# A build-time planner that tries eight orders of each step, and counts less time between engines

## The chip, the cores and the metric

The kernel runs on one core of a Trainium2 chip. The metric is the device time of one execution in microseconds: the median of several runs, 1663.62 us for the kernel before (four runs, 1661.84 to 1665.83 us). A core has a matrix engine (PE, TensorE), a vector engine (DVE, VectorE), an activation engine (ACT, ScalarE), a general engine (POOL, GpSimd) and a queue engine that starts DMAs (SP, SyncE). Each runs its own list of instructions strictly in order and waits on semaphores where it needs another's result. So the order in which the program puts the instructions on each engine decides who waits for whom.

## The reference

Linear attention without softmax, a norm of every row of 64, and then a mixture of four experts whose weights are given per row. All is in float32.

```python
kv = np.einsum('bhsd,bhse->bhde', k, v)        # B, H, S, D = 8, 8, 576, 64
out = np.einsum('bhsd,bhde->bhse', q, kv)
rms = np.sqrt(np.mean(out * out, axis=-1, keepdims=True) + 1e-06)
x = out / rms * g_norm                          # then (B,H,S,D) -> (B*S, H*D) = (4608, 512)
p = domain_probs / (domain_probs.sum(-1, keepdims=True) + 1e-09)
for e in range(4):                              # w1: (4, 512, 1024), w2: (4, 1024, 512)
    h = np.maximum(x @ w1[e], 0.0)
    out += p[:, e:e + 1] * (h @ w2[e])
```

## The kernel before

**The work.** The 4608 rows are cut into nine chunks of 512: the first 512 rows of each of the eight batches, and a ninth that gathers the last 64 rows of all of them. An expert times a chunk is a step, `s = e * 9 + c`, so there are 36 steps. A step multiplies up (rows by `w1[e]`, then a ReLU) and down (by `w2[e]`, then times the row's probability and added to the output). Both products are done in a Strassen-like scheme of seven products of halves instead of eight, applied once or twice, so DVE, POOL and ACT have to form sums and differences of blocks before and after. In expert 0 the attention of the next batch is worked in between: `key_values` (L999) forms kv, `attend` (L1024) multiplies by q, `turn_x` (L1069) transposes the normed rows with the help of an identity matrix. Step 0 is plain: `up_plain` (L1331) multiplies up without the scheme.

**The PSUM banks** matter here. PE writes only to PSUM, which is cut into eight banks: two each of the kinds `u1`, `u2`, `db` and `ab`. PE can't write a bank again before ACT or DVE have taken the previous result out of it. An up product of the scheme (L1244) writes `u1` or `u2` and is copied out by ACT (L1265) or added up by DVE (L1273). A down product writes `db` or `ab`, and ACT (L1409, L1579) or DVE (L1416, L1587) take it. `attend` needs two `ab` banks and two `db` banks at once; they are emptied by `evacuate` (L920 on DVE, L921 on ACT). `turn_x` needs both `ab` banks, emptied by ACT at L1081.

**The order.** None of this is written out in its final order. The kernel adds some 8,500 operations to a `Plan`, each with a key (its step and its place in the step), a cost for each engine that could do it, and the buffers that it reads and writes. `layout` then plays the program through at build time. At each moment it asks every engine that is free for an operation. On PE and SP the first ready one in order of the key is taken; on DVE, ACT and POOL the ready one with the earliest due time is taken. Due times run backwards from PE's order: what PE needs earlier is due earlier. An operation counts as ready only when every input has been finished for `CROSS` (0.3 us) if another engine made it, or for `SAME` (0.06 us) if the same one did; a bank or buffer is free again `CROSS` after its last use. The chip does not use these numbers: it waits on semaphores. They only shape the order. `layout` runs once.

**Fillers.** While the opening (batch 0's attention and the first loads) leaves PE without work, `layout` puts in idle pairs of transposes of the identity (L1715), two matmul instructions of 128 columns each. They compute nothing that is used. They are put only where the next real PE operation has a key below zero, which holds for the opening alone.

**The helper lines.** L410 is every half-array matmul of the scheme, L433 every sum or difference of blocks in SBUF, L439 every load.

Of the kernel before, what the change touches and what calls it, by code (L numbers as in the profile page):

```python
# [39 lines left out]
class Plan:  # L40
# [11 lines left out]
    CROSS, SAME, LANES = 0.3, 0.06, 8  # L52
# [5 lines left out]
    SLOW = 6.8  # L58
    SHARED, AHEAD, INORDER = ("big",), 0.3, ("xf",)
# [31 lines left out]
    def layout(self, slots, later, idle, idle_banks, idle_until):  # L91


        free = {k: [(0.0, i) for i in range(len(v))] for k, v in slots.items()}
        slots = {k: list(v) for k, v in slots.items()}
        later = list(later)
        live = {}
        for b in {b for op in self.ops for b in op.bufs}:
            live[b.kind] = live.get(b.kind, 0) + 1
        ended = {}  # L100
        todo = {e: [] for e in self.REACH}
        for n, op in enumerate(self.ops):
            op.n = n
            for e in op.cost:
                todo[e].append(op)
        for e in todo:
            todo[e].sort(key=lambda o: (o.key, o.n))
        keys, begun, spent = [], [], 0.0
        for op in todo["PE"]:
            keys.append(op.key)  # L110
            begun.append(spent)
            spent += op.cost["PE"]
# [8 lines left out]
        missing, after = {}, {op: [] for op in self.ops}  # L121
        for op in self.ops:
            missing[op] = len(op.deps)
            for d in op.deps:
                after[d].append(op)
        waiting = {k: {} for k in self.SHARED}

        def arm(op):
            for b in op.outs:
                if b.kind in waiting and b.slot is None and "SP" not in op.cost:  # L130
                    waiting[b.kind][op] = max([d.end for d in op.deps] or [0.0])

        for op in self.ops:
            if not missing[op]:
                arm(op)
        first, known = {k: {} for k in self.INORDER}, set()
        for op in self.ops:
            for b in op.outs:
                if b.kind in first and b not in known:
                    known.add(b)  # L140
                    first[b.kind][op] = True

        def claimed(kind, op):
            return sum(
                1 for o, since in waiting[kind].items()
                if o.due < op.due and since <= t + self.AHEAD and o is not op
            )

        busy = {e: 0.0 for e in todo}
        bus, port = 3.8, 0.0  # L150
        lanes = [0.0] * self.LANES
        t = 0.0
        wake = [0.0, 1.6]
        left = len(self.ops)
        order = []

        def ready(op, eng):
            when = 0.0
            for d in op.deps:
                if d.start is None:  # L160
                    return None
            for d in op.deps:
                when = max(when, d.end + (self.SAME if d.eng == eng else self.CROSS))
            need = {}
            for b in op.outs:
                if b.kind is not None and b.slot is None:
                    need[b.kind] = need.get(b.kind, 0) + 1
            for k, n in need.items():
                spare = self.SPARE.get(k, 0) if k != "xf" or op.key < self.FORMS else 0
                ahead = op.key > front + 0.1 and (eng == "SP" or op.early)  # L170
                if len(free[k]) < n + (spare if ahead else 0):
                    return None
                if k in waiting and len(free[k]) < n + claimed(k, op):
                    return None
                if k in first and any(o.due < op.due for o in first[k] if o is not op):
                    return None
                when = max(when, sorted(free[k])[n - 1][0])
            if eng == "SP":
                when = max(when, lanes[0])
            if op.port:  # L180
                when = max(when, port)
            return when

        while left:
            moved = False
            while todo["PE"] and todo["PE"][0].start is not None:
                todo["PE"].pop(0)
            front = todo["PE"][0].key if todo["PE"] else 1e9
            for eng in todo:
# [8 lines left out]
                best = None  # L198
                kept = {}
                for op in pending:  # L200
# [8 lines left out]
                    when = ready(op, eng)  # L209
# [9 lines left out]
                    best = op  # L219
                    if eng in ("PE", "SP"):  # L220
                        break
                if best is not None:
                    op = best
                    op.start, op.eng = t, eng
                    if eng == "SP":
                        busy[eng] = t + op.cost[eng]
                        bus = max(bus, t + 1.5) + op.kb / 215.0
                        op.end = bus + 0.5
                        lanes = lanes[1:] + [op.end]
                    else:  # L230
                        op.end = busy[eng] = t + op.cost[eng]
                        if op.kb:
                            op.end += 9.0 if op.kb == 512 else 8.0
                    if op.port:
                        port = op.end
                        heapq.heappush(wake, port)
                    for b in op.outs:
                        if b.kind is not None and b.slot is None:
                            free[b.kind].sort()
                            b.slot = free[b.kind].pop(0)[1]  # L240
                            b.ap = slots[b.kind][b.slot]
                    for held in list(waiting.values()) + list(first.values()):
                        held.pop(op, None)
                    for o in after[op]:
                        missing[o] -= 1
                        if not missing[o]:
                            arm(o)
                    for b in op.bufs:
                        b.left -= 1
                        if b.left == 0 and b.kind is not None:  # L250
                            end = max(o.end for o in [op] + b.readers + b.writers) + self.CROSS
                            free[b.kind].append((end, b.slot))
                            live[b.kind] -= 1
                            ended[b.kind] = max(end, ended.get(b.kind, 0.0))
                            for rule in [r for r in later if not any(live.get(k) for k in r[0])]:
                                later.remove(rule)
                                end = max(ended[k] for k in rule[0])
                                for ap in rule[2]:
                                    free.setdefault(rule[1], []).append((end, len(slots[rule[1]])))
                                    slots[rule[1]].append(ap)  # L260
                                heapq.heappush(wake, end)
                    heapq.heappush(wake, busy[eng])
                    heapq.heappush(wake, op.end + self.SAME)
                    heapq.heappush(wake, op.end + self.CROSS)
                    order.append(op)
                    left -= 1
                    moved = True
                if eng == "PE" and busy[eng] <= t and 1.6 <= t and front < idle_until:
                    kind, spare = next((
                        (k, f) for k in idle_banks for f in free[k] if f[0] <= t  # L270
                    ), (None, None))
                    if spare is not None:
                        took = 0.43 if t < self.SLOW else 0.23
                        op = Op(front, {"PE": took}, None, (), (), 0, False)
                        op.start, op.eng, op.end = t, eng, t + took
                        op.fn = lambda eng, bank=slots[kind][spare[1]]: idle(bank)
                        busy[eng] = op.end
                        free[kind].remove(spare)
                        free[kind].append((op.end, spare[1]))
                        heapq.heappush(wake, op.end)  # L280
                        order.append(op)
                        moved = True
            if moved:
                continue
            while wake and wake[0] <= t:
                heapq.heappop(wake)
            assert wake, ("no operation can start", t, left, {
                e: (todo[e][0].key, todo[e][0].fn) for e in todo if todo[e]
            }, {k: len(v) for k, v in free.items()})
            t = heapq.heappop(wake)  # L290
        self.length = max(o.end for o in order)
        return order
# [1473 lines left out]
```

## Time and profile before

| what | value |
|---|---|
| median of the runs | 1663.62 us |
| the profiled execution's own time | 1661.9 us |
| its span, first to last instruction | 1659.7 us |
| PE busy | 1650.9 us (99% of the span) |
| DVE busy | 1283.5 us (77%) |
| ACT busy | 976.3 us (59%) |
| POOL busy | 648.4 us (39%) |
| granted PE clock | 1.00 |

PE is busy nearly all the time, so the span is PE's work plus the time in which PE stands still. PE's work is the same set of products in any order; what an order can change is the fillers and the places where PE waits. "Start us, us" in a timeline are start and duration of a merged group of instructions of one line; a bracket tells how long the engine had been idle and what ended it. A matmul's duration reaches past the start of the next, since they overlap in the pipeline; so the time from one group's start to the next group's start is the better measure of what it costs.

### The profile page before, as it was taken

The page shows a single profiled execution, that of the slowest core. Times are in us where ns is not written, and L with a number is a line of the kernel's source. Part 1 is how long each engine was busy: PE and PEld are TensorE (multiplying, and loading weights), DVE is VectorE, ACT ScalarE, POOL GpSimd, SP SyncE. Part 2 cuts the span into 40 slices and gives each one's busy share as a digit, 9 for nine tenths or more (in the row PEclk, how much of TensorE's full clock was granted, in tenths as well). Part 3 has the DMA queues.
Part 4 walks back from the last instruction along what each step waited for, and adds up shares of the span by engine and source line. Part 5 has one row for each costly group of instructions (what it writes and reads, how often), then busy time and mean ns, then how long its engine had stood idle before and what let it go on. Part 6 is the DMA issues. An engine that isn't in the chain of part 4 may idle for free.

```text
span 1659.7 us, 66359 instructions
## 1 busy us (share of the span) xinstructions
PE 1650.9 (99%) x28884; PEld 1558.8 (94%) x28884; DVE 1283.5 (77%) x2153; ACT 976.3 (59%) x2420; POOL 648.4 (39%) x649
## 2 busy tenths in 40 slices
PE   9999999999999999999999999999999999999998
PEld 6688888888899999999999999999999999999996
DVE  4778777766888687888788887888888887788874
ACT  3455555554556665666666666666666666666662
POOL 3532323214344554333355445433355444433332
PEclk9999999999999999999999999999999999999999
DMA  9876865624466444444558444444577544444442
GB/s 215 192 227 183 228 181 145 167 101 181 160 175 149 112 117 119 115 114 113 141 161 194 115 117 118 103 116 117 137 185 179 129 116 117 106 114 116 117 104 52
DMA packets 208123, 234.27 MB, mean 141 GB/s; under 512 B 97368, under 2 KB 148440, under 8 KB 207832
## 3 DMA queue, kind: packets, MB, share of 16 engines
q1 hardware_dynamic: 184760, 193.32, 38.8%
q0 software_dynamic: 23072, 36.71, 14.6%
q8 instruction: 227, 3.72, 0.9%
q14 instruction: 64, 0.52, 0.1%
HBM read 155.79 MB, written 74.19 MB: 139 GB/s over the span
## 4 chain that ended last, share of the span: by engine, by line
PE 99%; DMA 0%; DVE 0%; ACT 0%; issue 0%; SPq 0%; ACTq 0%; DVEq 0%
PE u L410 48%; PE db L410 32%; PE ab L410 15%; PE ab L1004 1%; PE ab L1031 1%; PE ab L1072 1%; DMA big<-in_q_dram 0%; PE ab L1715 0%; PE db L1040 0%; PE ab L753 0%; PE ab L772 0%; PE ab L1093 0%; PE ab L817 0%; SPq L439 0%; DVE ss L944 0%
## 5 line engine op out<-in xcount | busy, mean ns | idle before, releaser
L433 DVE TENSOR_TENSOR big<-big,big 128x1024 f32<-128x1024 f32 (+1 forms) x518 | 503.1, 985 | 41.2 <-ACT big L1229 17.6
L410 PE MATMUL u<-xf,big 128*64 128x128 f32 x7072 | 507.9, 273 | 0.2
L410 PEld LDWEIGHTS u<-xf,big 128*64 128x64 f32 x7072 | 410.5, 137 | 5.7 <-issue 1.7
L410 PE MATMUL u<-xf,w1y 128*64 128x128 f32 x5304 | 384.1, 273 | 0.0
L410 PE MATMUL db<-big,big 128*64 128x128 f32 (+1 forms) x4320 | 361.1, 307 | 1.4 <-ACT snap L921 1.4
L1273 DVE TENSOR_TENSOR big<-u,snap 128x256 f32<-128x256 f32 x458 | 192.0, 421 | 174.3 <-PE u L410 137.5
L410 PEld LDWEIGHTS u<-xf,w1y 128*64 128x64 f32 x5304 | 308.9, 137 | 3.3 <-issue 0.3
L1265 ACT ACTIVATE snap<-u 128x256 f32<-128x256 f32 x490 | 188.0, 384 | 197.6 <-PE u L410 159.7
L410 PEld LDWEIGHTS db<-big,big 128*64 128x64 f32 x4320 | 265.0, 137 | 40.7 <-ACT snap L921 1.6
L433 POOL TENSOR_TENSOR big<-big,big 128x256 f32<-128x256 f32 (+1 forms) x166 | 196.9, 1190 | 156.4 <-DVE big L433 92.3
L1265 ACT ACTIVATE big<-u 128x256 f32<-128x256 f32 x458 | 175.0, 384 | 90.3 <-PE u L410 64.5
L433 POOL TENSOR_TENSOR big<-big 128x512 f32<-128x512 f32 (+1 forms) x79 | 94.8, 1201 | 148.7 <-DVE big L433 95.4
L1579 ACT ACTIVATE snap<-db 128x256 f32<-128x256 f32 (+1 forms) x230 | 82.4, 358 | 101.5 <-PE db L410 93.5
L1229 ACT ACTIVATE big<-big 128x1024 f32<-128x1024 f32 x131 | 137.7, 1051 | 5.5 <-DVE big L433 2.7
L433 DVE TENSOR_TENSOR big<-big 128x512 f32<-128x512 f32 (+1 forms) x128 | 111.3, 878 | 0.0
L1265 ACT ACTIVATE u<-u 128x256 f32<-128x256 f32 x245 | 91.0, 371 | 31.1 <-PE u L410 14.8
L1617 POOL TENSOR_TENSOR big<-big 128x512 f32<-128x512 f32 x28 | 35.7, 1276 | 184.3 <-DVE big L433 168.5
L1432 POOL DMA_DIRECT2D out_dram<-big x100 | 89.5, 1126 | 46.1 <-ACT big L1409 31.4
L410 PE MATMUL db<-small,big 128*64 128x128 f32 x1416 | 106.4, 273 | 0.4 <-ACT snap L1579 0.4
L1587 DVE TENSOR_TENSOR big<-ab,snap 128x256 f32<-128x256 f32 x160 | 67.2, 420 | 38.8 <-PE ab L410 25.6
L410 PE MATMUL ab<-big,big 128*64 128x128 f32 (+1 forms) x1344 | 93.6, 278 | 0.0
L410 PE MATMUL db<-kv,big 128*64 128x128 f32 x1264 | 87.4, 273 | 0.0
(193 smaller groups left out, 2343.3 us busy)
## 6 DMA issues: line engine op xcount, KB each, us to landing
xf<-x SPq DMA_DIRECT2D x108, 512.0 KB, 3.7
out_dram<-big POOLq DMA_DIRECT2D x84, 256.0 KB, 5.6
xf<-x_h SPq DMA_DIRECT2D x81, 256.0 KB, 3.3
xf<-x SPq DMA_DIRECT2D x81, 256.0 KB, 3.7
x<-xf SPq DMA_DIRECT2D x36, 512.0 KB, 4.7
big<-in_moe_w_dram SPq DMA_DIRECT2D x31, 512.0 KB, 5.3
x_h<-big SPq DMA_DIRECT2D x18, 512.0 KB, 4.1
big<-in_moe_w_dram POOLq DMA_DIRECT2D x17, 512.0 KB, 6.5
```

The costliest lines, as they stand in the source:

```text
L410: nc.tensor.matmul(out_[cols], lhsT=lhsT[:, cols], rhs=rhs, **kw)
L433: lambda eng: adder(eng).tensor_tensor(out=out_(), in0=a(), in1=b(), op=op),
L1004: nc.tensor.matmul(bank.ap[r * D:(r + 1) * D, o * D:(o + 1) * D], lhsT=ks[r], rhs=vs[r], start=(j == 0), stop=(j == len(sets) - 1), skip_g ...
L1031: nc.tensor.matmul(raw[r].ap[c * D:(c + 1) * D, (o * NR + t) * D:(o * NR + t + 1) * D], lhsT=qt.ap[half, col:col + D], rhs=kv.ap[half, o * ...
L1072: nc.tensor.transpose(turned[o].ap[:, r * P:(r + 1) * P], qt.ap[:, o * NT + r * P:o * NT + (r + 1) * P], ident[:])
L1229: lambda eng: nc.scalar.activation(out=b.ap[:], in_=b.ap[:], func=ACT.Relu),
L1265: lambda eng: nc.scalar.activation(out=where(), in_=ps.ap[:, 0:HN], func=ACT.Copy),
L1273: lambda eng: nc.vector.tensor_tensor(out=block(whole, a, t), in0=src.ap[:, 0:HN], in1=add_.ap[:], op=ALU.add),
L1432: nc.gpsimd.dma_start(out=dst, in_=cell(i)[parts, :], accum_op=ALU.add)
L1579: lambda eng: nc.scalar.activation(out=where(), in_=group_of(ps.ap), func=ACT.Copy),
L1587: lambda eng: nc.vector.tensor_tensor(out=cell(tq, dq), in0=group_of(src.ap), in1=group_of(add_.ap), op=ALU.add,),
L1617: lambda eng: adder(eng).tensor_tensor(out=whole(to), in0=whole(a), in1=whole(b), op=ALU.add),
```

## The change

Three things. `CROSS` goes from 0.3 to 0.2 us. `layout` no longer runs once: at each of the steps it saves its state, plays this step and the next eight times, and keeps the play in which PE stood still least (the planner's clock less the real PE work done, `self.t - self.worked`; fillers are not counted as work). Play 0 uses the due times as they are; plays 1 to 7 add to each due time of this step's and the next step's operations a random number of mean 0 and spread 1 us. Then the step is played once more with the chosen numbers, and the next step is searched. And for this the body of `layout` is moved into methods that can be stopped and restarted (`ready`, `claimed`, `run`, `begin`, `arm`). The rules of readiness, PE's "first ready in order of the key" and the costs are as before. No instruction of the chip is new, and nothing but the order, the buffers that operations get, the engine that an operation with a choice goes to, and the count of fillers can differ.

```diff
-    CROSS, SAME, LANES = 0.3, 0.06, 8
+    CROSS, SAME, LANES = 0.2, 0.06, 8
...
+    TRIES, LOOK, SPREAD = 8, 1, 1
...
+        for op in self.ops:
+            op.base = op.due
...
+        steps = {}
+        for op in self.ops:
+            steps.setdefault(math.floor(op.key), []).append(op)
+        for step in sorted(steps):
+            begin = self.save()
+            tried = []
+            for n in range(self.TRIES):
+                draw = random.Random(100 * n + step)
+                for op in steps[step] + steps.get(step + 1, []):
+                    op.due = op.base + (draw.gauss(0.0, self.SPREAD) if n else 0.0)
+                if self.run(step + 1 + self.LOOK):
+                    tried.append((self.t - self.worked, n))
+                self.restore(begin)
+            n = min(tried)[1]
+            draw = random.Random(100 * n + step)
+            for op in steps[step] + steps.get(step + 1, []):
+                op.due = op.base + (draw.gauss(0.0, self.SPREAD) if n else 0.0)
+            assert self.run(step + 1)
+        self.run(math.inf)
...
+    def run(self, until):
...
+            front = todo["PE"][0].key if todo["PE"] else 1e9
+            if front >= until:
+                return True
...
+    def begin(self, op, eng):
...
+        if eng == "PE":
+            self.worked += op.cost[eng]
```

## The prediction

> **What bounds the kernel now.** I read the page first: span, busy times, and the chain that ended last.
>
> ```profile
> span 1659.7 us, 66359 instructions
> PE 1650.9 (99%) x28884; PEld 1558.8 (94%) x28884; DVE 1283.5 (77%) x2153; ACT 976.3 (59%) x2420; POOL 648.4 (39%) x649
> PE 99%; DMA 0%; DVE 0%; ACT 0%; issue 0%; SPq 0%; ACTq 0%; DVEq 0%
> ```
>
> PE is the chain: 8.8 us of the span are not PE's. The busy times by stretch of time tell where these 8.8 us lie (second number of a row: PE).
>
> ```profile
> 0.00:16.00 16.00, 13.79 (x228) 12.05 (x230) 2.80 (x9) 6.26 (x13) 0.70 (x6) 1.00 0.93 221
> 16.00:32.00 16.00, 16.00 (x176) 9.20 (x170) 12.10 (x26) 5.55 (x14) 9.91 (x7) 1.00 0.89 222
> 32.00:66.00 34.00, 32.59 (x388) 15.76 (x388) 20.65 (x47) 13.77 (x39) 19.26 (x19) 1.00 0.99 206
> 66.00:120.00 54.00, 54.00 (x875) 44.65 (x876) 42.98 (x95) 28.37 (x71) 16.78 (x24) 1.00 0.80 219
> 120.00:1600.00 1480.00, 1479.65 (x26456) 1431.04 (x26454) 1173.59 (x1931) 901.26 (x2236) 587.42 (x581) 1.00 0.53 138
> 1600.00:1660.00 60.00, 54.88 (x780) 46.06 (x776) 31.42 (x48) 21.11 (x51) 14.29 (x12) 1.00 0.32 63
> ```
>
> 2.2 us are in the first 16 (the identity and the loads), 1.4 before 66, 0.35 in the 1480 us of the body, 5.1 at the end. Of the last, some 4.4 are the last sums and the output's DMA behind PE's last product. After the opening the waits of PE name two places:
>
> ```profile
> PE db L410 <- ACT snap L921: 1.4, 1, 1.4
> PE db L410 <- ACT snap L1579: 0.4, 1, 0.4
> ```
>
> Waits below 0.15 us beyond the pipeline's overlap are in no such list, so I also compared start to start. A scheme product takes 0.44 us from its start to the next one's. Where it is longer, PE waited:
>
> ```profile
> 179.78 0.66 PE L410 MATMUL u<-small,big 128*64 128x128 f32 x8
> 180.27 0.61 PE L410 MATMUL u<-xf,big 128*64 128x128 f32 x8
> 180.93 0.33 PE L410 MATMUL u<-small,big 128*64 128x128 f32 x2
> ```
>
> 180.27 to 180.93 is 0.66, so 0.22 of waiting. Four such places (147.1, 180.9, 251.3, 519.9 us) come to 0.22 + 0.22 + 0.30 + 0.21 = 0.95 us, and the place of 0.4 in the list is 0.54 by this measure (1628.85 to 1629.83 less 0.44). With the 1.42 at 61.3 us, **PE's waiting behind the opening is 2.9 us**. The last item that an order can change is filler work, which counts as busy:
>
> ```profile
> L1715 PE MATMUL ab<-ident 128*128 128x128 f32 x60 | 9.6, 316 | 1.4 <-POOL ident masks.py:199 1.4
> 30.87 1.31 PE ab L1715 x12
> ```
>
> Even a perfect order can't gain more than the 2.9 and the fillers behind the first real product. That bounds the gain at some 6 us, 0.36%. About 0.2% (3.3 us) is what a measurement of this kernel can tell from no change.
>
> **Part 1: fillers.** Both builds' orders are known before a run. The kernel before has 31 filler pairs (62 matmuls), the one after has 24 (48). The nine ahead of the first product are kept. The clearest loss is the block of twelve matmuls at 30.87 us, ahead of the second half of `up_plain`: PE waited there for ACT to take the last `turn_x` of batch 0 out, while one first-half product of `up_plain` (1.7 us) had already been spent. After, that product is placed behind the last `turn_x` and covers ACT's 0.69 us copy, so the block is gone. Fourteen matmuls at 1.31 / 12 = 0.109 us are **-1.53 us**. What covers this: the loads of `w1` must be there 1.5 us earlier. They land between 18.9 and 24.7 us; the first is needed at 21.5, the last not before 37, so the cover holds. If it did not, the fillers' time would turn into waiting, and the term would be 0.
>
> [...] I take -1.53.
>
> **Part 2: where PE will wait.** A product that reuses a bank has to wait for the round PE, ACT, PE. From the trace: a product placed at 144.35 is followed by the next at 144.78 and its ACT copy starts at 145.01, so 0.22 us from PE's slot to ACT; a copy ends at 145.69 + 0.37 and PE starts at 146.11, so 0.05 from ACT to PE. With a copy of 0.38 a bank is free 0.65 us after its product. In the order before, six PE operations stand less than 0.65 us of PE work behind the product whose bank or block they need, and five of the waits above are at these. In the order after there are seven, and most are others. Each, with durations from this trace:
>
> - `turn_x` of batch 1 is now directly followed by `attend` of its second half, which needs both `ab` banks. ACT first has two ReLU copies (0.22 + 0.66 from the start of `turn_x`), then two L1081 copies, 1.27 for both, and 0.05. That is 2.20, less 1.03 of `turn_x`: **1.17**.
> - That `attend`, then one product, then the first down product, which needs `db`. ACT starts 0.10 before `attend`'s end and does one copy (0.63 to the next), then two small ones (0.26, 0.27): 1.06, and 0.05, less 0.44: **0.67**. This takes the place of the 1.42.
> - A down product directly behind the user of its bank: 0.22 + 0.48 + 0.05: **0.75**.
> - `attend` of batch 2, one product, `turn_x`: DVE's copy of 0.69 starts 0.03 behind `attend`; 0.77 less 0.44: **0.33**.
> - `attend` of batch 4, directly followed by a down product on `db`: the 1.11 of the second item, uncovered: **1.11**.
> - The end of the last step but one, as before: **0.54** for two of the seven.
>
> The rows behind the `attend` items are these (L1031, L1040 are `attend`, 1.32 us from start to next start):
>
> ```profile
> 198.17 1.16 PE L1031 MATMUL ab<-kv,small 64*64 64x64 f32 x64
> 199.16 0.40 PE L1040 MATMUL db<-kv,small 64*64 64x64 f32 x8
> 199.39 0.60 ACT L921 ACTIVATE small<-ab 128x512 f32<-128x512 f32 x1 [0.68 <-PE ab L1031]
> 199.49 0.66 PE L410 MATMUL u<-xf,big 128*64 128x128 f32 x8
> 199.52 0.69 DVE L920 COPY small<-ab 128x512 f32<-128x512 f32 x1 [0.83 <-PE db L1040]
> 200.02 0.27 ACT L921 ACTIVATE snap<-db 64x128 f32<-64x128 f32 x1
> ```
>
> To these I add 0.5 us for waits through two engines (as at 147.1 before, where DVE's L944 was late), for which I see some five candidates and take 0.1 each, with 0 and 1.5 as ends. Sum 1.17 + 0.67 + 0.75 + 0.33 + 1.11 + 0.54 + 0.5 = 5.1, against 2.9 before: **+2.2 us**.
>
> **Part 3: the smaller count between engines.** 0.3 + 0.38 + 0.3 = 0.98 us kept a reuse of a bank three products away (1.31); 0.2 + 0.38 + 0.2 = 0.78 allows two (0.87). PE operations with less than 0.9 us of PE work behind their producer go from 80 to 343. The real round is 0.65, so each has 0.22 us to spare, and behind the waiting PE everything is queued. What eats the 0.22 is an ACT or DVE that is still at something else, such as a ReLU of 1.05 us (L1229). Before, none of the 74 such places that had these 0.22 us shows a wait. From none in 74 to 263 new ones: between 0 and some 11 waits of 0.2, so 0 to 2.2 us; I take **+0.3**, near the row that shows none. DVE, ACT and POOL have 376 us and more to spare in the span; that their work moves costs nothing beyond these waits. SP's loads are put by the same rules: before, no load made PE wait behind 16 us, and the closest ones after 60 us landed 0.2 us ahead of DVE. The order after keeps the same kinds of loads as the closest; 0, with -0 and +1 as ends.
>
> **The sum.** -1.53 + 2.2 + 0.3 = +1.0 us. The profiled execution's 1661.9 (span 1659.7 and 2.2 around it) becomes 1662.9. The median of the runs lies 1.7 above that execution, so the forecast is **1664.6 us**, no change that can be told.
>
> **The rivals.**
>
> *Faster (1659.8).* The planner's choice works: fillers -1.7, and the new waits shrink to some 0.8 since ACT takes the small `db` copies first. For it: the search counts just this idle time, and the real round is 0.13 below what even the new count supposes. Against: PE takes the first ready operation by key in all eight plays, so the search moves only the other engines, and the seven close places stand in the order as built. -1.7 - 2.1 = -3.8.
>
> *Slower (1669.5).* The two-product spacing fails in the repeating part. Steps 10 to 35 have much the same order, so a place where ACT is late is late in every step. Its place is the L1265 copy behind an L1229 ReLU, its price 0.2 us times 26 = 5.2 us; beside my +1.0 less 0.3 that is 1669.5. It decides from 2.4 us on, that is 0.09 us a step. For it: 263 places more with only 0.22 to spare. Against: no such wait before; ACT is busy 59%.
>
> *The change doesn't do what it says.* The planner's idle time is not the chip's: 0.98 of planned round against 0.65 real made it count waits that never were. Then it trades nothing for nothing, 1663.6; this falls into "no change".
>
> **How the numbers follow.** My forecast with the third rival: 0.67. Faster by over 0.2% (below 1660.3): 0.09. Slower by over 0.2% (above 1666.9): 0.24, the larger since one repeating wait is multiplied by 26. The range reaches from -3 (fillers -1.7, waits 2 shorter than summed, a median that falls 0.5 low) to +5.4 (the upper ends of parts 2 and 3, or the repeating wait): 1660.6 to 1669.0.
>
> **What would show it.** Right: 48 L1715 matmuls; the second half of `up_plain` starting near 30.5 instead of 32.1 us; PE waits named by L1081 and L921 or L920 between 55 and 65 us and near 200; body idle of 4 to 6 us start to start, none repeating by step. Wrong: PE waits on L1265 in step after step; a PE wait for a load; the granted clock below 1.00.

## The result and the profile after

The kernel after takes **1660.69 us** (median; 1659.57 to 1664.75), the kernel before, run beside it, 1662.79 (1660.89 to 1665.83). The ratio is 0.9988 with an interval of 0.9984 to 0.9992: **2.1 us less, between 1.3 and 2.7**. It is just inside the range (1660.6 to 1669.0) and still under the 0.2% that was named as the limit of what can be told, but its interval doesn't reach 1, and it points the other way than the forecast of +1.0. The time lies nearer to the rival "faster" (1659.8) than to the forecast (1664.6).

In the profile after, every line number of the kernel is 64 higher: L474 is the scheme's product (L410 before), L985 and L1145 are ACT's copies (L921, L1081), L1329 is ACT's copy of an up product (L1265), L1779 the fillers (L1715). First the page: span, busy times, and the chain that ended last.

```profile
span 1660.5 us, 66193 instructions
PE 1649.2 (99%) x28870; PEld 1557.1 (94%) x28870; DVE 1248.1 (75%) x2142; ACT 980.2 (59%) x2421; POOL 704.6 (42%) x659
PE 98%; DVE 1%; DMA 0%; ACT 0%; issue 0%; SPq 0%; POOL 0%; POOLq 0%; DVEq 0%; ACTq 0%
```

This execution (1662.37 us) is one of the longer ones of the kernel, and its span is longer than that of the one before (1659.7), while the medians say the opposite. One profile of each would have told the wrong sign. What can be read from it: PE's busy time is 1.7 us less, most of which is the fourteen fillers; DVE works 35 us less and POOL 56 us more, and neither has more than 1% of the chain. Busy times by stretch of time (the columns of the first such table; PE is the second number):

```profile
0.00:16.00 16.00, 14.15 (x220) 12.21 (x220) 2.10 (x8) 6.30 (x13) 0.70 (x6) 1.00 0.94 229
66.00:120.00 54.00, 52.84 (x870) 44.09 (x868) 42.87 (x91) 28.43 (x69) 24.39 (x28) 1.00 0.80 222
120.00:1600.00 1480.00, 1477.90 (x26426) 1428.57 (x26424) 1135.69 (x1923) 903.17 (x2235) 641.44 (x589) 1.00 0.53 138
```

PE stands still 1.2 us between 66 and 120 and 2.1 between 120 and 1600, where it had stood 0 and 0.35. The list of its waits, whole lines of that view, says for whom:

```profile
PE u L474 <- issue: 1.3, 1, 1.3
PE db L474 <- ACT snap L985: 1.1, 2, 0.8
PE db L474 <- ACT big L1473: 0.7, 1, 0.7
PE ab L1095 <- ACT big L1145: 0.7, 2, 0.4
PE ab L1136 <- DVE small L1017: 0.5, 1, 0.5
PE db L474 <- ACT snap L1643: 0.5, 1, 0.5
```

Most of the names are those that the prediction gave; L1017, on DVE, is not, and its 0.5 us are not in the list of `again`, the same order once more. The first line is a new kind, "issue": PE waited for nothing that the profile shows. A timeline of PE has its place:

```profile
145.46 0.27 PE L474 MATMUL u<-small,big 128*64 128x128 f32 x1
147.00 0.55 PE L474 MATMUL u<-small,big 128*64 128x128 f32 x6 [1.27 <-issue]
```

In the middle of a product, between two of its eight matmuls, 1.27 us are lost. Another execution of the same order (`again`, below) has no such wait in its list, so it belongs to the execution and not to the order. Without it, this profile's span would be 0.5 us under that of before.

### The profile page after: what moved, and what is told of

Same layout as the page of the kernel before. It is cut to its first block, busy times and chain, and to the rows that moved or that the text cites. A ratio compares the mean times of both kernels' runs of the same rounds, so it can differ in the third digit from the quotient of the medians.

```text
span 1660.5 us, 66193 instructions
## 1 busy us (share of the span) xinstructions
PE 1649.2 (99%) x28870; PEld 1557.1 (94%) x28870; DVE 1248.1 (75%) x2142; ACT 980.2 (59%) x2421; POOL 704.6 (42%) x659
## 4 chain that ended last, share of the span: by engine, by line
PE 98%; DVE 1%; DMA 0%; ACT 0%; issue 0%; SPq 0%; POOL 0%; POOLq 0%; DVEq 0%; ACTq 0%
PE u L474 47%; PE db L474 32%; PE ab L474 15%; PE ab L1068 1%; PE ab L1095 1%; PE ab L1136 1%; DMA big<-in_moe_w_dram 0%; PE ab L1779 0%; PE ab L817 0%; DVE big L497 0%; PE db L1104 0%; PE ab L1157 0%; DVE rt L700 0%; PE ab L836 0%; PE ab L881 0%
## 5 line engine op out<-in xcount | busy, mean ns | idle before, releaser
L497 DVE TENSOR_TENSOR big<-big,big 128x1024 f32<-128x1024 f32 (+1 forms) x544 | 515.4, 965 | 29.4 <-ACT big L1293 12.0
L474 PE MATMUL u<-xf,big 128*64 128x128 f32 x7072 | 513.0, 273 | 0.1
L474 PEld LDWEIGHTS u<-xf,big 128*64 128x64 f32 x7072 | 412.0, 137 | 5.4 <-issue 0.8
L474 PE MATMUL u<-xf,w1y 128*64 128x128 f32 x5304 | 393.3, 273 | 0.0
L474 PE MATMUL db<-big,big 128*64 128x128 f32 (+1 forms) x4280 | 359.2, 308 | 2.2 <-ACT snap L985 1.1
L1337 DVE TENSOR_TENSOR big<-u,snap 128x256 f32<-128x256 f32 x470 | 197.4, 421 | 204.1 <-PE u L474 153.8
L474 PEld LDWEIGHTS u<-xf,w1y 128*64 128x64 f32 x5304 | 310.9, 137 | 3.3 <-issue 0.8
L474 PEld LDWEIGHTS db<-big,big 128*64 128x64 f32 x4280 | 261.8, 137 | 43.2 <-issue 2.3
L1329 ACT ACTIVATE snap<-u 128x256 f32<-128x256 f32 x490 | 188.2, 384 | 189.1 <-PE u L474 165.3
L497 POOL TENSOR_TENSOR big<-big,big 128x256 f32<-128x256 f32 (+1 forms) x158 | 218.4, 1385 | 166.8 <-DVE big L497 72.8
L1329 ACT ACTIVATE big<-u 128x256 f32<-128x256 f32 x470 | 179.5, 384 | 64.3 <-PE u L474 38.4
L497 POOL TENSOR_TENSOR big<-big 128x512 f32<-128x512 f32 (+1 forms) x104 | 126.9, 1221 | 182.4 <-DVE big L497 110.1
L1293 ACT ACTIVATE big<-big 128x1024 f32<-128x1024 f32 x136 | 143.0, 1051 | 5.2 <-DVE big L497 4.4
L1329 ACT ACTIVATE u<-u 128x256 f32<-128x256 f32 x245 | 90.9, 371 | 38.4 <-PE u L474 26.2
L474 PE MATMUL db<-small,big 128*64 128x128 f32 x1312 | 98.7, 273 | 0.0
L474 PE MATMUL ab<-big,big 128*64 128x128 f32 (+1 forms) x1360 | 94.8, 278 | 0.0
L1473 ACT ACTIVATE big<-big,p_all 128x256 f32<-128x256 f32 x180 | 85.5, 501 | 0.4 <-POOL big L1681 0.2
L474 PE MATMUL ab<-kv,big 128*64 128x128 f32 x1232 | 85.1, 273 | 0.0
```

Source lines behind the costliest of these rows:

```text
L474: nc.tensor.matmul(out_[cols], lhsT=lhsT[:, cols], rhs=rhs, **kw)
L497: lambda eng: adder(eng).tensor_tensor(out=out_(), in0=a(), in1=b(), op=op),
L1293: lambda eng: nc.scalar.activation(out=b.ap[:], in_=b.ap[:], func=ACT.Relu),
L1329: lambda eng: nc.scalar.activation(out=where(), in_=ps.ap[:, 0:HN], func=ACT.Copy),
L1337: lambda eng: nc.vector.tensor_tensor(out=block(whole, a, t), in0=src.ap[:, 0:HN], in1=add_.ap[:], op=ALU.add),
L1473: lambda eng: nc.scalar.activation(out=cell(i, half), in_=ap(), func=ACT.Copy, scale=prob()),
```

## The experiments

Two profiles of one order differ by more than the effect (1662.37 us for `after`, 1659.88 for `again`), so two measures stand beside each other: medians of many runs, and a **ledger** from the traces. For the ledger each matmul's time to the next one's start is compared with the usual spacing of its form; what is beyond that, and every filler, is time lost to PE. Here "the opening" is the first 17 us of real work, and "the repeating part" is 300 to 1600. A loss is booked by how much real work PE had done by then, so that different orders are compared at the same stage. 17 us of real work are done near 29 us of the clock; the block of twelve fillers lies in "17-24". Neighbouring columns are exact to some 0.3 us only, since a change from one form of matmul to another can fall on either side of an edge; the sums don't depend on this. `body_only`, `refill` and `seed2` are left out, since their clock fell back for a while (last section); for `measured32` none was made.

```
real work done, us:   0-17  17-24  24-300  300-1600  1600-end   sum
before               12.24   1.58    6.13      1.01      0.76   21.7
neither              12.24   1.58    5.96      1.00      0.76   21.5
look_b               12.72   1.58    6.29      1.01      0.76   22.4
noblock              12.51   0.27    6.34      1.00      0.76   20.9
after (less 1.27)    11.91   0.00    7.98      0.53      0.84   21.3
again                11.04   0.00    7.64      0.53      0.84   20.1
look_a               11.55   0.00    7.33      0.53      0.84   20.3
look_a2              12.11   0.00    7.51      0.53      0.84   21.0
cross_only           13.20   0.00    7.51      3.42      0.84   25.0
search_only          13.10   1.58    6.36      0.67      0.76   22.5
open_only            11.62   0.00   11.17      0.83      0.76   24.4
c25                  10.83   0.00    7.36      2.80      0.84   21.8
nofill               12.30   0.00    9.44      0.53      0.84   23.1
tries32              11.68   0.00    8.13      0.55      0.84   21.2
```

Medians of the timed runs, with the ratio to the kernel before on the same chip (ratios are formed within rounds, so they needn't be the quotient of the medians):

```
              count  orders   median     before     ratio  [95%]
neither        0.3     1      1662.30    1662.42    0.9998 [0.9989, 1.0007]
cross_only     0.2     1      1664.08    1662.42    1.0008 [1.0000, 1.0017]
search_only    0.3     8      1662.19    1662.42    0.9992 [0.9984, 1.0001]
again          0.2     8      1660.33    1662.42    0.9986 [0.9978, 0.9995]
open_only      mixed   8      1663.03    1662.87    0.9997 [0.9988, 1.0006]
body_only      mixed   8      1663.33    1662.87    0.9999 [0.9990, 1.0008]
refill         0.2     8      1663.61    1662.87    1.0003 [0.9994, 1.0012]
c25            0.25    8      1663.64    1662.87    0.9998 [0.9990, 1.0007]
seed2          0.2     8      1661.56    1662.46    0.9997 [0.9989, 1.0006]
nofill         0.2     8      1660.45    1662.46    0.9988 [0.9980, 0.9997]
tries32        0.2     32     1662.26    1662.46    0.9997 [0.9989, 1.0006]
measured32     by pair 32     1661.41    1662.46    0.9992 [0.9983, 1.0000]
```

### The two halves of the change

All four corners of "smaller count" and "search". `neither` is the new code with both switched off; its order is that of the kernel before.

```diff
-    CROSS, SAME, LANES = 0.2, 0.06, 8
+    CROSS, SAME, LANES = 0.3, 0.06, 8
...
-    TRIES, LOOK, SPREAD = 8, 1, 1
+    TRIES, LOOK, SPREAD = 1, 1, 1
```

> The changed code with both numbers set back: 0.3 us between engines, one play per step. Its order is that of the kernel before, instruction by instruction. Both theories: 1662.8 us, within 0.5 of the kernel before. Its profile is a second look at that order: if the places where TensorE waits (61.3, 147, 181, 251, 520, 1630 us, 3.0 us in sum by start to start) are set by the order, they come back to within 0.3 us; what does not come back is chance of one execution.

Measured 1662.30 against 1662.42: the rewriting of `layout` into methods moves nothing that can be told. The trace also tells how exact such a comparison is. Waits of the order come back in the same place with the same length to 0.02 us (near 61, 181, 251, 520, 648 and 1630 us), while the loss in the first 17 us of work varies between executions of the same order, 12.24 to 12.72 us in the old one and 11.04 to 12.11 in the new one (the ledger above).

`cross_only` has the smaller count and one order (`TRIES` 1).

```diff
-    TRIES, LOOK, SPREAD = 8, 1, 1
+    TRIES, LOOK, SPREAD = 1, 1, 1
```

> 0.2 us between engines, one play per step. 24 filler pairs as in the changed kernel, 363 places with under 0.9 us of TensorE work behind a producer, 14 of them under 0.45 us (the changed kernel: 343 and 7). Theory A, the smaller count is the gain: 1660.7 us or within 0.6 of it. Theory B, the search is the gain and the smaller count alone only makes waits: seven more places under 0.45 us at 0.2 to 1.1 us each, so 1662.5 to 1665.

1664.08, at or above the kernel before (ratio 1.0000 to 1.0017) and 3.75 us above `again`. Its ledger has what the whole change has from 17 to 300 us (no block of fillers, 7.5 us in "24-300"), but 3.42 us in the repeating part instead of 0.53. Two lines of its list of PE's waits, and a timeline of PE:

```profile
PE u L474 <- ACT big L1329: 0.5, 1, 0.5
PE u L474 <- ACT small L1329: 0.5, 1, 0.5
```

```profile
905.60 0.64 PE L474 MATMUL u<-xf,big 128*64 128x128 f32 x8
906.77 1.09 PE L474 MATMUL u<-xf,w1y 128*64 128x128 f32 x16 [0.53 <-ACT small L1329]
```

From 905.60 to 906.77 are 1.17 us where a product takes 0.44, so 0.73 of waiting; it comes with another 0.22 at 910.1, and the pair again near 1293 and 1296 us, in steps 19 and 28. So the wait on the up product's copy that the rival "slower" is about exists, but in two steps and not in 26. In the kernel after, PE runs through at this stage, 0.44 us from each start to the next:

```profile
906.91 0.61 PE L474 MATMUL u<-xf,w1y 128*64 128x128 f32 x8
907.35 0.61 PE L474 MATMUL db<-small,big 128*64 128x128 f32 x8
907.78 0.61 PE L474 MATMUL u<-xf,big 128*64 128x128 f32 x8
```

`search_only` has the old count and eight orders.

```diff
-    CROSS, SAME, LANES = 0.2, 0.06, 8
+    CROSS, SAME, LANES = 0.3, 0.06, 8
```

> 0.3 us between engines, eight plays per step. 31 filler pairs and 75 places under 0.9 us, as before the change. Theory A (the smaller count): 1662.8 us, no gain, since the fillers stay. Theory B (the search): 1660.7 to 1661.5.

1662.19: 0.2 less by the medians, 1.3 by the ratio, whose interval reaches 1.0001. The block of fillers is still there (1.58); the repeating part goes from 1.01 to 0.67. `again` is the kernel after, unchanged.

> The changed kernel unchanged, for a second profile. In its first profile TensorE stood still for 1.27 us at 147.0 us in the middle of one product, with nothing named that ended it. If that is an accident of one execution it is gone, and the profiled execution takes 1660.7 to 1661.2 us instead of 1662.4; if the order makes it, it is there again and 1662.4 stands. Median 1660.7 either way.

1660.33, the gain once more. The corners don't add: +1.7 for the smaller count and -0.2 (or -1.3) for the search would be +1.5 (or +0.4), and both together give -2.1. The intervals of `cross_only` and `again` lie apart (1.0000 to 1.0017 and 0.9978 to 0.9995), so under the tighter plan the search is worth its 3.75 us beyond the noise. Within the tighter plan the search takes away the waits that the tighter plan makes: PE operations with less than 0.45 us of PE work behind what they wait for are 14 in `cross_only` and 7 in the kernel after, and the repeating part falls by 2.9 us. (`search_only`'s trace doesn't have the waits near 520 and 648 us either, so the search took these away at the old count too.)

### Opening or body?

Then two theories stood. **O**: the gain is the opening's (fewer fillers, a better order there). **S**: it is the spacing in the steps behind. `open_only` gives the smaller count to the opening alone, `body_only` to the steps from 0 on alone. (The due times are worked out ahead of all steps, with 0.3 in the first and 0.2 in the second.)

```diff
+            self.CROSS = 0.2 if step < 0 else 0.3
```

> Eight plays; 0.2 us between engines while the planner is in the opening (keys below zero), 0.3 after. 24 filler pairs as in the changed kernel, but 75 places under 0.9 us of TensorE work, as before the change. Theory O, the gain is the opening's alone (from the profiles so far: about -2.1 us by the start of step 0's second half), the body costs what it did: 1660.3 us, ratio 0.9988 or lower. Theory S, the close spacing in the body is a part of the gain: 1661.5 to 1662.4.

```diff
+            self.CROSS = 0.3 if step < 0 else 0.2
```

> Eight plays; 0.3 us in the opening, 0.2 after. 31 filler pairs as before, 345 places under 0.9 us. Theory O: no gain or a loss, 1662.4 to 1663.5 us. Theory S: 1660.7 to 1661.5.

Neither shows a gain: 1663.03 and 1663.33 against 1662.87, ratios 0.9997 and 0.9999. Neither theory holds alone. In `open_only` the opening is as good as in the kernel after (11.62 and no block), but "24-300" has 11.17 us instead of 7.6. Its list of PE's waits (line numbers one more than in the kernel after) shows waits that the kernel after doesn't have:

```profile
PE db L475 <- POOL big L498: 1.5, 1, 1.5
PE db L475 <- ACT snap L986: 1.3, 2, 0.9
PE ab L1069 <- DMA kv<-in_v_dram: 0.6, 1, 0.6
PE ab L1137 <- DVE small L1018: 0.6, 1, 0.6
```

A likely reading is that a PE that leaves the opening earlier meets sums on POOL and DVE and a load that are not earlier, and gives the time back in the first steps; no run separates this from what else differs in that order. In `body_only` the block of fillers is kept, as all 31 pairs are, and the median shows no gain from the steps behind it.

`refill` puts the removed block back into the kernel after: six filler pairs ahead of the second half of `up_plain`. It adds work that nothing uses.

```diff
...
+    for _ in range(6):
+        more = Op(0.0, {"PE": 0.23}, lambda eng: idle(slots["ab"][1 - busy]), (), (), 0, False)
+        more.eng = "PE"
+        order.insert(at, more)
```

> The changed kernel with six filler pairs (twelve matmuls) put back ahead of the second half of up_plain, where the kernel before has them. If they are pure cost: +1.31 us, 1661.7. If TensorE has to wait there anyway (for ACT's copy of the last turn_x, or for w1): up to 1.31 us of it is hidden, 1660.4 to 1661.

1663.61, ratio 1.0003 (0.9994 to 1.0012) where the kernel after stands at 0.9988: the six pairs cost between 1 and 4 us. That they would be hidden is out; the 1.31 us that they last fit. (In the new order a product stands between the last `turn_x` and these fillers, so they had nothing to bridge here; whether they bridge anything in the old order is asked below.) `c25` sets the count to 0.25.

```diff
-    CROSS, SAME, LANES = 0.2, 0.06, 8
+    CROSS, SAME, LANES = 0.25, 0.06, 8
```

> The changed kernel with 0.25 us between engines. 24 filler pairs, 60 places under 0.9 us of TensorE work. Theory O: 1660.3 to 1660.8, as the changed kernel or better. Theory S: 1661.5 to 1662.4.

1663.64, no gain. It has no block either, and the best opening of all (10.83), but 2.80 us in the repeating part. The gain doesn't grow steadily as the count gets smaller.

### One draw, or the method?

`seed2` is the kernel after with other random numbers.

```diff
-                draw = random.Random(100 * n + step)
+                draw = random.Random(100 * n + step + 5000)
...
```

> The changed kernel with other random numbers for plays 1 to 7. 24 filler pairs, 355 places under 0.9 us of TensorE work, 11 under 0.45 us (changed kernel 343 and 7; the smaller count without a search 363 and 14). If the search helps by whatever draw: 1660.3 to 1661 us. If it helps only as far as it removes close places, so by the luck of the draw: between the two, 1661.5 to 1663.

`nofill` is the kernel after without the fillers behind PE's first real product (fifteen pairs are left out, which compute nothing that is used).

```diff
+    first = next(n for n, o in enumerate(order) if o.eng == "PE" and o.outs)
+    order = [o for n, o in enumerate(order) if n < first or o.eng != "PE" or o.outs]
```

> The changed order without the 15 filler pairs that stand behind the first real product; the nine ahead of it stay. The pairs take 30 x 0.109 = 3.3 us of TensorE. If they only fill time in which TensorE would wait anyway: 1660.4, no change. If some stand in the way (the opening is TensorE's own chain in part of the executions): 1658.5 to 1660. If they keep the clock up: a granted clock of 0.5 for 3.4 us or more ahead of 35 us in the profile, and 1662 to 1665.

`tries32` tries 32 orders of each step, and `measured32` (32 orders too) counts by pair of engines what the traces show in the place of one number, and a PSUM bank as free 0.06 us after its last use.

```diff
-    TRIES, LOOK, SPREAD = 8, 1, 1
+    TRIES, LOOK, SPREAD = 32, 1, 1
```

> The changed kernel with 32 plays of each step in place of eight. 24 filler pairs, 350 places under 0.9 us, 7 under 0.45 us. If more search removes more real waits: 1658.5 to 1660. If what is left is set by the order of keys on TensorE, which no play changes: 1660.3 +- 0.5.

```diff
+    def cross(self, a, b):
+        if a == b:
+            return self.SAME
+        if b == "POOL":
+            return 0.22 if a == "PE" else 0.1
+        return 0.22 if a == "PE" else self.CROSS if a in ("SP", "POOL") else 0.06
...
```

> 32 plays, and the count between engines taken from the trace by pair: 0.22 us from TensorE, 0.06 to TensorE and between ACT and DVE, 0.1 to POOL, 0.2 from loads and POOL. 24 filler pairs, 409 places under 0.9 us, 6 under 0.45 us. If a count nearer to the chip lets the search see the real waits: 1658 to 1659.5. If 0.13 us to spare in each round was what kept the chip from waiting: waits on L1329 in step after step, 1662 to 1666.

`seed2` has 0.9 us less than before by the medians, `tries32` 0.2, `measured32` 1.05. Only the last one's interval stops at 1.0000, those of the first two go past it. None is above the kernel before, but 2.1 us are shown for one draw only: four times as many orders did not do better than eight, and truer counts did not beat the kernel after. The intervals overlap with that of the kernel after, so how much is the method and how much the luck of the draw stays open. The repeating part speaks for the method: counted the same way it is some 0.9 us in `seed2` and 0.7 in `body_only` (the fall of the clock is over by then), both far from the 3.42 without a search. `c25`, with 2.80, speaks against it. `nofill` is equal to the kernel after (1660.45; 0.9988). Its list of PE's waits shows why:

```profile
PE ab L836 <- DMA big<-in_v_dram: 3.9, 4, 1.3
PE ab L941 <- DVE small L984: 1.6, 1, 1.6
```

Where fillers stood, PE waits for the loads of the opening. The fifteen pairs that the change leaves behind the first product cost nothing, unlike the six that it took away.

### Was the removed block pure cost?

Then the orders of before and after once more, to see how far single executions spread, and the order of before with nothing but the block taken out. `noblock` leaves out six filler pairs.

```diff
...
+    at = next(n for n, o in enumerate(order) if o.eng == "PE" and o.outs and o.outs[0].name == "up0_0"
+              and o.key >= 0.0)
+    gone = [n for n in range(at) if order[n].eng == "PE" and not order[n].outs][-6:]
+    order = [o for n, o in enumerate(order) if n not in gone]
```

> The order of before (the new code with 0.3 us and one play) without the block of six filler pairs ahead of the second half of up_plain, which takes 1.58 us there by its profile. If the fillers were the cost, the second half starts 1.58 us earlier. If they only fill the wait for ACT's copy of the last turn_x (0.22 + 0.69 + 0.05 = 0.96 us), it starts 0.6 us earlier and a wait of about 0.9 us on ACT stands in their place; then the changed order's gain there comes of putting another product in the place, not of leaving fillers out.

> Another look at the order of before: TensorE's time beyond its real work by the start of the sixteenth of its microseconds was 12.24 us in both looks so far. If the opening sets it, 12.2 again, up to 1.5 more with a late clock or an instruction stall.

> Another look at the changed order: the same measure was 11.91 and 11.04. If the changed opening is shorter ahead of the filler block too, 11.0 to 11.9, below 12.2. If that was chance of the clock's start, about 12.2.

> As the look before it: 11.0 to 11.9 if the changed opening is shorter, about 12.2 if not. The wait of 1.27 us in the middle of a product at 147 us, there in the first profile of this order and not in the second, is there in neither of the two or in one of them if it is an accident.

Single executions: `noblock` 1661.14, `look_b` (order of before) 1662.55, `look_a` and `look_a2` (order of after) 1660.07 and 1660.83, and the kernel before beside them 1662.20. A timeline of PE in `neither`, the order of before:

```profile
30.21 0.66 PE L881 MATMUL ab<-ident,big 128*128 128x128 f32 x4
30.71 1.47 PE L1779 MATMUL ab<-ident 128*128 128x128 f32 x12
32.11 3.23 PE L474 MATMUL u<-big,big 128*64 128x512 f32 x14
```

and in `noblock`, with ACT's copy that the fillers were to bridge, from a timeline of ACT:

```profile
30.49 0.66 PE L881 MATMUL ab<-ident,big 128*128 128x128 f32 x4
31.07 4.51 PE L474 MATMUL u<-big,big 128*64 128x512 f32 x20
```

```profile
31.18 0.69 ACT L889 ACTIVATE big<-ab,gcol 128x512 f32<-128x512 f32 x1 [3.48 <-PE ab L881]
```

From the start of the transposes to the product were 1.90 us and are 0.58. The product begins at 31.07, before the copy at 31.18 has even begun. In the kernel a product of `up_plain` goes over two parts of its input block, and only the second part is what this copy brings: its first four of eight matmuls, 0.215 us each, read the part that was already there, and the fifth is due at 31.93, when the copy has ended (31.87). The planner counts a block as one thing and waits for all of it, so it saw a gap of 1.3 us on PE and filled it. The ledger of `noblock` falls from 1.58 to 0.27 at this place and keeps that (20.9 in sum). In this execution the block was not cover but **1.31 us of loss**.

## Why the prediction was wrong

The four executions of the order of after, less the 1.27, average 20.6 us in the ledger; the three of the order of before, 21.9. The difference by term:

```
                                      forecast    ledger
opening, up to and with the block       -1.53      -2.33
waits between 24 and 300                +2.2       +1.49
repeating part, 300 to 1600             +0.3       -0.48
the end                                  0         +0.08
sum                                     +1.0       -1.24   (medians: -2.1, -2.7 to -1.3)
```

Two landmarks give the same: the second half of `up_plain` starts at 32.3 us on average before and at 30.1 after, 2.2 less; from there to the start of PE's last matmul are 1622.8 and 1623.7 (less the 1.27), 1.0 more. So the forecast had the shape right, a gain in the opening and new waits behind it, and the sign of the sum wrong. **The step that failed is the cost of the waits behind the opening: +2.5 in parts 2 and 3, and +1.0 to +1.1 in the traces.** Half of that miss lies in the repeating part, where the search was at work, to which the forecast gave no term.

**The base: 0.8 us high.** "The median of the runs lies 1.7 above that execution" rested on four runs. With sixty the median of before is 1662.79, 0.9 above it.

**Part 1: the right size, for a reason that was half true.** There are 48 fillers as forecast, so fourteen fewer at 0.109 us, -1.53: twelve are the block (1.31), two stand ahead of it. The second half of `up_plain` starts at 30.3 us in the profile after, forecast near 30.5. The new order does put a product in ACT's way, as the forecast says, but `noblock` shows that the fillers covered almost nothing, since PE could have started. The clock took nothing of this term: in the profile after the granted clock stays at 1.00 from its rise at 7.44 us to 1659.49, behind PE's last product (1656.09), and in `nofill` with fifteen pairs fewer still (mean 1.000) it didn't fall either.

The other 0.7 to 0.8 us of the opening, booked at nothing, are as large as a stop that no wait explains. In each of the three profiles of the old order PE stops near 16 us under "issue", ahead of the last matmul of the third L772 product (L836 in the new code), for 0.28, 0.51 and 1.62 us, 0.80 on average. None of the four profiles of the new order has such a stop there. `refill`, which has the same opening, stopped for 0.92 us, and `noblock`, with the old opening, for 0.59. So the stop can come in both orders; whether it is rarer in the new one, these nine profiles don't tell.

**Part 2: the side after was right, the side before too small.** Start to start in `again`, the seven places have 0.99 for 1.17, 0.51 for 0.67, 0.84 for 0.75, 0.15 for 0.33, 0.84 for 1.11, 0.77 for 0.54 and some 0.8 in all for the waits through two engines (0.5): 4.9 us for the forecast 5.1. Two of them, as the timeline of PE in the profile after has them:

```profile
60.33 0.66 PE L474 MATMUL u<-big,big 128*64 128x128 f32 x8
61.28 1.95 PE L474 MATMUL db<-big,big 128*64 128x256 f32 x16 [0.29 <-ACT snap L985]
67.78 1.95 PE L474 MATMUL db<-big,big 128*64 128x256 f32 x16 [0.67 <-ACT big L1473]
```

The term that was too small is "PE's waiting behind the opening is 2.9 us". Measured the same way all along the traces of `before` and `neither`, it is some 3.3: the wait at 61.3 is 1.48 and the one at 147.1 about 0.3, and two at 648.5 (0.15) and 1630.8 us (0.11) were passed over. So by this list the waits grow by 1.6 and not by 2.2; the ledger, which adds up everything behind the opening, has 1.1.

**Part 3: the sign was wrong.** "Between 0 and some 11 waits of 0.2 ... I take +0.3": in the kernel after no wait for L1329 is in the list, and the repeating part loses 0.5 us less than before. Most of these 0.5 are two waits of the old order, the 0.22 near 519.9 us, which the forecast had counted in its 2.9, and the 0.15 near 648.5; the new order doesn't have them. The first, in a timeline of PE in the profile before (0.65 from start to start where 0.44 is usual):

```profile
519.24 0.61 PE L410 MATMUL u<-xf,w1y 128*64 128x128 f32 x8
519.89 0.66 PE L410 MATMUL u<-xf,big 128*64 128x128 f32 x8
```

What failed is the sentence under the rival "faster", that "the search moves only the other engines, and the seven close places stand". The seven places do stand, and they cost about what was forecast. But moving ACT and DVE is just what removes waits on ACT: with the same smaller count and no search, the repeating part has 3.42 us, with it 0.53. These 2.9 us are most of the 3.75 between `cross_only` and `again`, and the forecast gave the search nothing. Its +1.0 was near to what the smaller count does alone (+1.7).

**What stays open.** The ledger gives -1.2 and the medians -2.1, and 0.7 to 0.8 of the ledger's part is the stop that may be chance. The ledger rests on three and four executions that spread by a microsecond, so the rest isn't assigned. One rival can be set aside: the clock falls back for a while in some executions (last section), but among those whose mean granted clock is 1.000 the medians are 1660.57 for the kernel after (35 executions) and 1662.41 for the kernel before (69, those run beside the experiments), so the gain isn't the clock's.

## What to carry to other kernels

When two edits work on one plan, cost them as a pair: here the tighter count made waits and the search removed them, and neither alone showed a gain. Before believing that a filler or a wait covers something, look at when the next instruction's own inputs were there; a planner that takes a block as one thing sees gaps that the chip hasn't. For an effect of 0.1% compare medians, and use traces only for what recurs from execution to execution to a hundredth of a microsecond.

## What the runs showed of the hardware

**The start of the fast clock varies.** All of these kernels send the same fillers from 1.4 us on, and yet in eighteen profiles the granted clock reached 1.00 between 4.66 us (`look_a2`) and 7.44 us (`after`). (The share in the rows by stretch of time counts only from there on, so the row 0.00:16.00 shows 1.00.) In the profile before it rose at 4.67 us, and the fillers stand 0.213 us apart ahead of that and 0.109 behind it. What sets the moment, none of these runs tests.

**It can fall back in the opening.** In three profiles (`body_only`, `refill`, `seed2`) the clock went to half 10.24 us after it had risen, for 3.41, 3.41 and 6.83 us; in `refill` its mean from 17 to 21 us is 0.58, in `seed2` from 17 to 24 us 0.51. Busy times by stretch for the last 3.41 us of `body_only` and `seed2` ahead of the fall, and for the stretch as long after the rise in `search_only`, where the clock did not fall (PE is the second number, the granted clock the third from the right):

```profile
13.97:17.38 3.41, 1.82 (x34) 1.45 (x35) 2.05 (x7) 1.30 (x4) 0.00 (x0) 1.00 1.05 321
13.74:17.15 3.41, 2.05 (x38) 1.40 (x30) 2.05 (x7) 1.74 (x6) 0.00 (x0) 1.00 1.07 285
13.12:16.53 3.41, 2.03 (x52) 1.59 (x42) 2.05 (x7) 1.71 (x5) 0.00 (x0) 1.00 1.09 261
```

In `refill` PE was busy 1.85 of the last 3.41 us ahead of the fall. The longest stop that began there was 1.48, 1.10 and 0.92 us (`body_only`, `seed2`, `refill`, all under "issue"), and PE was still busy more than half of the stretch. In the other fifteen profiles, cut into stretches of 3.41 us from the rise on, PE was busy 2.03 us or more in each up to 35 us. So 1.82 to 2.05 us of work in the last 3.41 (53 to 60%) is what the three falls have in common; with 2.03 and no fall in `search_only`, no limit can be read from this, and what makes the clock fall is not shown.

**PE stops in the middle of a product, for nothing named.** Fifteen of the eighteen profiles have stops under "issue" of 0.3 to 1.6 us, mostly at 14 to 17 us and near 145 to 150, as the 1.27 shown above. Whether PE was waiting for its instructions is not shown. The 16 KB packets of the instruction queue run through the whole trace (227 in the profile of before, one in some 7 us, and one in 4 us near 145), so one that runs near a stop proves nothing, and no run here tests it.
